# A mixture of experts whose weights' sums leave GpSimd and are kept in DRAM, with the first expert's first layer as a plain product

## The chip, the cores and the metric

The kernel runs on one core of one Trainium2 chip. The metric is device time in microseconds (us), the median of several executions. One further execution was taken with the hardware profiler; its span, from the first instruction to the last, is what the profile's rows divide. The engines are named as in the profile: PE is TensorE (PEld its loads of weights), DVE VectorE, ACT ScalarE, POOL GpSimd, SP the queue that issues DMAs.

## The reference

Attention over q, k, v (4 batches, 8 heads, 1152 positions, 64 features), with the queries averaged in pairs, gives 2304 tokens of 512 features. They go through a dense mixture of eight experts (each 512 to 1024 to 512) and then through a second mixture, a soft one with 32 slots.

```python
def _moe_ref(x, w_gate, w1, w2):
    N, D = x.shape                      # 2304, 512
    E = w_gate.shape[1]                 # 8
    logits = x @ w_gate
    P = np.exp(logits - logits.max())
    for _ in range(8):
        P /= P.sum(1, keepdims=True) + 1e-09
        P /= P.sum(0, keepdims=True) + 1e-09
        P *= N / E
    out = np.zeros((N, D), dtype=np.float32)
    for e in range(E):
        h = np.maximum(x @ w1[e], 0.0)  # 512 -> 1024
        ye = h @ w2[e]                  # 1024 -> 512
        out += P[:, e:e + 1] * ye
    return out
```

All values are float32. The kernel computes each large product from a high and a low half of both operands (three matmuls: high x high, high x low, low x high). Making the halves is called a split: ScalarE casts the high half (`hi`, L459, or L519, L634), VectorE subtracts it for the low half (`lo`, L462, or L520, L635).

## The kernel before

**Attention** runs first, over 32 heads in 288 slots of nine to a head (18 slots are a pair of heads). ScalarE's exponentials are L221, GpSimd adds up their rows (L227), and L244, L246 and L250 to L260 normalise. A table `hooks` puts other work at numbered slots, counted back from attention's end: in the kernel before, parts of `prep` (sums and splits of the tokens, whose results are stored in DRAM), sums and splits of expert 0's weights, and `v_store`, which makes sums of expert 0's second weights and stores them.

**The first mixture** has nine blocks of 256 tokens, eight of them in four pairs u = 0 to 3 and one single, u = 4, taken in the order 0, 1, 4, 2, 3. For experts 0 to 6 both layers are products in Strassen's manner: a pair's first layer is made of seven products of forms of w1 (11, 12, S2, S3, 22, S1, S4, of which S1 to S4 are sums of w1's quarters) with forms of the tokens (B11 to B22, T1 to T4, read back from DRAM by `load_x`, L565, into three buffers). Each is two chunks of 12 matmuls (`chunk`, L661). A block's second layer is seven products of 12 matmuls (`product`, L706) of forms of the hidden values (`h_sum`, L628, `h_split`, L634 and L635) with seven forms of w2 (V, j = 0 to 6). L718 multiplies by the gate's P and adds to the output. L670, L680, L684 and L689 bring the first layer's products out of PSUM. The last expert is plain in both layers (`g1`, L737 to L739, and `g2`).

The order is written out by hand: a list `items` of chunks and products, which are TensorE's steps, and `at(k, ...)`, which puts other engines' work behind step k, with `late` as its order there. `merge` writes a stretch of steps from a text ("c" a chunk, "p" a product): a pair's chunks stand among the products of the block before, then six chunks stand together, then the rest stand among the products of the pair's first block. `starts[e, u]` is a pair's first step, `bounds[e, u]` (r) the last of its six chunks together. Each engine works through its own queue in order, SP's DMAs included.

**Weights at a change of expert.** While pair u = 3 of expert e runs, `stage_w` and `stage_v` load the eight quarters of expert e+1's weights into the staging buffers (pool `stg`, five of 4 KB a partition); GpSimd makes four sums of w1 (`w_sum`, L452) and four of w2 (`v_sum`, L483) in place, and each form is split into its tile behind the last matmul of the expert before that reads that tile. The splits lie at steps r-8 to r+36. GpSimd also makes two of the four `h_sum`s of each block.

Of the kernel before, what the change touches and what calls it, by code (L numbers as in the profile page):

```python
# [357 lines left out]
def tile_attention__moe__softmoe(ctx, tc, q, k, v, w_gate, w1, w2, phi, m2_w1, m2_w2, out):  # L358
# [105 lines left out]
    def w_hi(e, form):  # L464
        Wt[e, form] = w_tile(form)
        hi(Wt[e, form], staged[e, HOME[form]])

    def w_lo(e, form):
        lo(Wt[e, form], staged[e, HOME[form]])

    def w_split(e, form):
        w_hi(e, form)
        w_lo(e, form)
# [6 lines left out]
    def v_sum(e, k, eng=None):  # L480
        q = [staged[e, x] for x in ((0, 0), (0, 1), (1, 0), (1, 1))]
        dst, a, b = {1: (q[0], q[1], q[0]), 2: (q[0], q[3], q[0]), 3: (q[1], q[3], q[1]), 4: (q[2], q[2], q[0])}[k]
        (eng or nc.vector).tensor_tensor(out=dst, in0=a, in1=b, op=ALU.subtract)  # L483

    VHOME = [(0, 0), (1, 0), (0, 0), (0, 0), (0, 1), (1, 1), (1, 0)]
    Vd = {}

    def v_store(k):
        v_sum(0, k)
        j = {1: 3, 2: 2, 3: 4, 4: 6}[k]  # L490
        Vd[j] = dram_p.tile([128, 1024], F32, name=f"vd{j}")
        nc.sync.dma_start(out=Vd[j], in_=staged[0, VHOME[j]])

# [3 lines left out]
    def v_hi(e, j):  # L497
        if e:
            V[e, j] = v_tile(j)
        hi(V[e, j], staged[e, VHOME[j]])  # L500

    def v_lo(e, j):
        lo(V[e, j], staged[e, VHOME[j]])

    def v_raw(j, t):
        staged[0, j] = t
        if j in Vd:
            nc.sync.dma_start(out=t, in_=Vd[j])
        else:
            nc.sync.dma_start(out=t.rearrange("p (c d) -> p c d", c=4), in_=quarter(0, VHOME[j]))  # L510

    def v0_split(j):
# [813 lines left out]
```

## Time and profile before

| | us |
|---|---|
| median of three executions | 2233.35 |
| lowest and highest | 2231.29, 2235.98 |
| the profiled execution | 2234.42 |
| its span, first to last instruction | 2232.6 |

The mean granted clock of TensorE in the span is 0.982 of full speed. Times within the span are counted from its start. A matmul's recorded length holds its way through the array, so matmuls overlap in the rows: the pace is read from one start to the next.

### The profile page before, as it was taken

The numbers are of one execution on the slowest core, as the hardware profiler recorded it, in microseconds if no ns is written. First come the engines' busy times: TensorE is split into PE (matmuls) and PEld (weight loads), VectorE is DVE, ScalarE is ACT, GpSimd is POOL, SyncE is SP. The second block draws the span as 40 slices with busy tenths as digits, with TensorE's granted clock in tenths as the row PEclk, the third lists the DMA queues.
The fourth block names the chain that finished last, engine by engine and source line by source line (L and its number), as shares of the span: only waits on it lengthen the run. The fifth ranks groups of instructions, "written<-read, shape, count | busy, mean of one in ns | idle before, by whom it ended". The sixth has DMA issues, their size and how long they took to land.

```text
span 2232.6 us, 40083 instructions
## 1 busy us (share of the span) xinstructions
PE 2124.9 (95%) x16119; PEld 1899.6 (85%) x16119; DVE 1448.3 (65%) x2421; ACT 971.8 (44%) x1994; POOL 724.3 (32%) x479
## 2 busy tenths in 40 slices
PE   7999999999999999999999999999999999999997
PEld 5677666666899899989999999999999999999863
DVE  5878787885666865785576478557647745544461
ACT  3555555555544543443344344345434534311232
POOL 5888786777011411331141133114113311000000
PEclk9999999999999999999999999999999999999998
DMA  8745656524344322422333242233224223487568
GB/s 205 179 117 150 163 142 182 128 67 144 123 174 152 116 98 77 142 95 76 133 114 105 76 142 95 77 132 123 95 85 137 97 80 110 169 323 257 208 225 266
DMA packets 153065, 311.49 MB, mean 140 GB/s; under 512 B 47920, under 2 KB 86832, under 8 KB 150832
## 3 DMA queue, kind: packets, MB, share of 16 engines
q1 hardware_dynamic: 152880, 308.93, 43.7%
q8 instruction: 128, 2.10, 0.4%
q14 instruction: 57, 0.47, 0.1%
HBM read 250.69 MB, written 25.17 MB: 124 GB/s over the span
## 4 chain that ended last, share of the span: by engine, by line
PE 69%; DVE 20%; ACT 5%; issue 3%; DMA 1%; SPq 1%; POOL 1%; ACTq 0%; DVEq 0%; POOLq 0%
PE y L706 20%; PE g L661 12%; PE seed L661 9%; PE o L234 5%; PE se L218 5%; DVE ho L635 5%; PE S L189 4%; ACT ho L634 2%; DVE v L462 2%; DVE acc L718 2%; DVE w L462 2%; DVE m L190 2%; DVE hr L689 1%; PE g L738 1%; PE g L739 1%
## 5 line engine op out<-in xcount | busy, mean ns | idle before, releaser
L706 PE MATMUL y<-v,ho 128*128 128x256 f32 x5292 | 704.5, 288 | 47.6 <-DVE acc L718 33.4
L706 PEld LDWEIGHTS y<-v,ho 128*128 128x128 f32 x5292 | 669.6, 195 | 61.2 <-issue 33.8
L661 PE MATMUL g<-xs,w 128*128 128x256 f32 x3360 | 442.7, 284 | 0.0
L661 PEld LDWEIGHTS g<-xs,w 128*128 128x128 f32 x3360 | 422.4, 193 | 1.4 <-issue 1.3
L227 POOL TENSOR_TENSOR acc<-acc,e 128x576 f32<-128x576 f32 x224 | 329.1, 1469 | 70.8 <-ACT e L221 60.2
L628 POOL TENSOR_TENSOR ht<-hr,ht 128x512 f32<-128x512 f32 x63 | 84.9, 1347 | 685.0 <-DVE ho L635 679.6
L635 DVE TENSOR_TENSOR ho<-ht,ho 128x512 fp32r<-128x512 f32 x252 | 232.6, 925 | 107.9 <-ACT ho L634 105.4
L190 DVE TENSOR_REDUCE m<-S 128x1 f32<-128x384 f32 x432 | 229.7, 547 | 74.3 <-PE S L189 61.7
L635 DVE TENSOR_TENSOR ho<-hr,ho 128x512 fp32r<-128x512 f32 x189 | 162.5, 860 | 162.8 <-ACT ho L634 162.6
L718 DVE SCALAR_TENSOR_TENSOR acc<-y,P,acc 128x256 f32<-128x256 f32 x378 | 181.1, 480 | 133.1 <-PE y L706 131.2
L221 ACT ACTIVATE e<-se 128x288 f32<-128x288 f32 x576 | 207.1, 412 | 96.7 <-PE se L218 89.5
L661 PE MATMUL seed<-xs,w 128*128 128x256 f32 x2016 | 247.7, 283 | 0.0
L661 PEld LDWEIGHTS seed<-xs,w 128*128 128x128 f32 x2016 | 244.2, 192 | 0.8 <-ACT v L459 0.4
L218 PE MATMUL se<-q,kd 128*128 128x288 f32 x1152 | 223.5, 312 | 7.2 <-ACT e L221 5.7
L218 PEld LDWEIGHTS se<-q,kd 128*128 128x128 f32 x1152 | 179.1, 192 | 21.0 <-ACT e L221 14.5
L634 ACT CAST ho<-ht 128x512 fp32r<-128x512 f32 x252 | 149.5, 615 | 104.9 <-DVE ht L628 71.3
L628 POOL TENSOR_TENSOR ht<-hr 128x512 f32<-128x512 f32 x63 | 84.2, 1337 | 300.5 <-ACT hr L670 300.5
L234 PE MATMUL o<-e,vr 128*64 128x288 f32 x1152 | 174.0, 424 | 0.0
L189 PE MATMUL S<-kd,q 128*128 128x384 f32 x384 | 150.0, 395 | 18.1 <-DVE m L190 16.4
L670 ACT ACTIVATE hr<-hr 128x512 f32<-128x512 f32 x112 | 69.9, 632 | 201.6 <-DVE hr L689 201.6
L189 PEld LDWEIGHTS S<-kd,q 128*128 128x128 f32 x384 | 74.3, 194 | 82.3 <-issue 31.9
L684 ACT COPY hr<-seed 128x512 f32<-128x512 f32 x112 | 65.8, 587 | 158.0 <-PE seed L661 157.9
(182 smaller groups left out, 2580.4 us busy)
## 6 DMA issues: line engine op xcount, KB each, us to landing
stg<-in_moe_w_dram SPq DMA_DIRECT2D x64, 512.0 KB, 6.0
xs<-xd0B SPq DMA_DIRECT2D x37, 512.0 KB, 3.2
xs<-xd1B SPq DMA_DIRECT2D x37, 512.0 KB, 3.3
xs<-xd2B SPq DMA_DIRECT2D x37, 512.0 KB, 3.3
xs<-xd3B SPq DMA_DIRECT2D x37, 512.0 KB, 3.6
kd<-kp SPq DMA_DIRECT2D x32, 576.0 KB, 6.3
xs<-xd0T SPq DMA_DIRECT2D x28, 512.0 KB, 3.3
xs<-xd1T SPq DMA_DIRECT2D x28, 512.0 KB, 3.2
```

Source lines behind the costliest of these rows:

```text
L189: nc.tensor.matmul(ps, lhsT=w, rhs=r[:, 384 * n:384 * n + 384], start=True, stop=True)
L190: nc.vector.tensor_reduce(out=M_[ph][:, x, n:n + 1], in_=ps, axis=AX.X, op=ALU.max)
L218: nc.tensor.matmul(ps, lhsT=kd[:, z, 128 * c:128 * c + 128], rhs=y[:, h, g], start=z == 0, stop=z == 1)
L221: nc.scalar.activation(out=e[:, g], in_=ps, func=AF.Exp, scale=1.0 / 16)
L227: nc.gpsimd.tensor_tensor(out=acc_[ph], in0=acc_[ph], in1=e, op=ALU.add)
L234: nc.tensor.matmul(O_[ph][64 * g:64 * g + 64, :288], lhsT=raws["v"][pi][:, h, c, :], rhs=E_[ph, c][:, g], start=c == 0, stop=c == 8,)
L628: (eng or nc.vector).tensor_tensor(out=o, in0=a, in1=b, op=op)
L634: nc.scalar.copy(o[:, 0], p)
L635: nc.vector.tensor_tensor(out=o[:, 1], in0=p, in1=o[:, 0].bitcast(F32), op=ALU.subtract)
L661: nc.tensor.matmul(o, lhsT=w[:, a, kk, cols], rhs=x[:, b, kk], start=begin, stop=kk == 1 and z == 2, skip_group_check=not first or f2 > 0,)
L706: nc.tensor.matmul(ps, lhsT=o[:, x, c], rhs=v[:, w, c], start=first and c + z == 0, stop=c + z == 5, skip_group_check=not first,)
L718: nc.vector.scalar_tensor_tensor(out=y, in0=ps, scalar=p, in1=y, op0=ALU.mult, op1=ALU.add)
```

## The change

- GpSimd does no sums in the first mixture. `h_sum` s3 and s4 go to VectorE, each put one step or less ahead of its split.
- The eight sums of an expert's weights are made an expert ahead, on VectorE (`fsum`): for expert e+1 while pairs u = 1 (w1) and u = 2 (w2) of expert e run (for expert 1, in blocks 5 to 7 of expert 0). They are stored in DRAM (`fstore`). At the change of expert all 14 forms are loaded one by one (`stage_f`), the sums from DRAM and the others as they are.
- The splits of the 14 forms are spread over r-8 to r+31 by a table (`FORMS`, and `FORMS0` for expert 1): load, high half and low half each have a step.
- Expert 0's first layer is one plain product (`plain`, four steps of 24 matmuls a block), from a plain split of its weights in four parts (`p_split`; part 0 in attention, 1 to 3 behind it) and of the tokens (`x0_split`, per block, whose halves are also stored as B11 to B22). Blocks follow one another, a block's four steps among the seven products of the block before.
- Attention's hooks keep only the load and split of one part of the weights, `x0_split(0)`, three more loads and the load of the gate's weights. T1 to T4 and BD are made in expert 0's blocks 1 to 4 and 7; expert 0's seven forms of w2 from four raw quarters in its first eight slots; the gate's steps lie in the slots of expert 0, with one more step between a row sum and its column sum.
- The staging pool has four buffers for five, the pool of token and output tiles ten for nine.

```diff
@@ pools, sums and splits
-    xa_p = ctx.enter_context(tc.tile_pool(name="xa", bufs=NBLK))
-    stg_p = ctx.enter_context(tc.tile_pool(name="stg", bufs=5))
+    xa_p = ctx.enter_context(tc.tile_pool(name="xa", bufs=NBLK + 1))
+    stg_p = ctx.enter_context(tc.tile_pool(name="stg", bufs=4))
...
-    def w_sum(e, name, eng=None):
-        q = {x: staged.get((e, x)) for x in W1Q}
+    Fd = {}
+
+    def fsum(e, name):
         dst, a, b, op = {
             "S3": ("11", "11", "21", ALU.subtract),
             "S1": ("21", "21", "22", ALU.add),
-            "S2": ("11", "22", "11", ALU.subtract),
-            "S4": ("12", "12", "11", ALU.subtract),
+            "S2": ("22", "22", "11", ALU.subtract),
+            "S4": ("12", "12", "22", ALU.subtract),
+            3: ((0, 0), (0, 1), (0, 0), ALU.subtract),
+            4: ((0, 1), (1, 1), (0, 1), ALU.subtract),
+            2: ((1, 1), (1, 1), (0, 0), ALU.subtract),
+            6: ((1, 0), (1, 0), (1, 1), ALU.subtract),
         }[name]
-        (eng or nc.vector).tensor_tensor(out=q[dst], in0=q[a], in1=q[b], op=op)
+        t = staged[e, dst]
+        nc.vector.tensor_tensor(out=t, in0=staged[e, a], in1=staged[e, b], op=op)
+        staged[e, name] = t
+
+    def fstore(e, name):
+        d = Fd[e, name] = dram_p.tile([128, 1024], F32, name=f"fd{e}{name}")
+        nc.sync.dma_start(out=d, in_=staged[e, name])
+
+    def stage_tile(e, name):
+        if name in (0, "S4"):
+            return xa_p.tile([128, 1024], F32, tag="xa", name="stg")
+        return stg_p.tile([128, 1024], F32, tag="stg", name="stg")
+
+    def stage_f(e, name):
+        if (e, name) in Fd:
+            t = staged[e, name] = stage_tile(e, name)
+            nc.sync.dma_start(out=t, in_=Fd[e, name])
+        elif name in VQ:
+            stage_v(e, VQ[name], stage_tile(e, name))
+            staged[e, name] = staged[e, VQ[name]]
+        else:
+            stage_w(e, name)
...
+    def x0_split(i):
+        u, t = divmod(i, 2)
+        for h in range(2):
+            pool, tag, bufs = (m_p, "hr", 4) if i and h else (wp_p, "x", 3)
+            x = X0[i, h] = pool.tile([128, 2, 2, 256], F32R, tag=tag, name="xs", bufs=bufs)
+            z = x.rearrange("p z k n -> p z (k n)")
+            part = xa[i].rearrange("p k n -> p (k n)")[:, 512 * h:512 * h + 512]
+            nc.scalar.copy(z[:, 0], part)
+            nc.vector.tensor_tensor(out=z[:, 1], in0=part, in1=z[:, 0].bitcast(F32), op=ALU.subtract)
...
@@ attention's hooks
-    for h, step, fs in ((-210, 8, prep(0)), (-134, 4, prep(1)), (-36, 8, X2[:4])):
-        for n, f in enumerate(fs):
-            hooks[h + step * n] = [f]
-            hooks[h + step * n + 2] = [store_x]
-    for h, f in {
...
-        -102: lambda: [stage_w(0, q) for q in ("22", "11", "21", "12")],
-        -92: lambda: w_split(0, "11"),
-        -88: lambda: w_sum(0, "S3"),
-        -80: lambda: w_split(0, "S3"),
-        -72: lambda: w_sum(0, "S1"),
-        -64: lambda: w_sum(0, "S2"),
-        -56: lambda: w_split(0, "S2"),
-        -48: lambda: w_split(0, "12"),
-        -40: lambda: w_sum(0, "S4"),
-        -24: lambda: load_x(3),
-        -286: lambda: [stage_v(0, q) for q in Q],
-        -276: lambda: v_store(1),
-        -266: lambda: v_store(3),
-        -256: lambda: v_store(2),
-        -246: lambda: v_store(4),
-    }.items():
+    PTAG = ("S3", "22", "S1", "S4")
...
+            {-56: [lambda: stage_p(0, 0)],
+             -48: [lambda: p_split(0, 0, PTAG[0])],
+             -40: [lambda: x0_split(0)],
+             -24: [lambda: stage_p(0, 1), lambda: stage_p(0, 2), lambda: stage_p(0, 3)],
...
@@ the plain first layer
+    def plain(i, fp):
+        ps = pg.tile([128, 512], F32, tag="g", name="g")
+        w = Wt[0, fp].rearrange("p z (k f) -> p z k f", k=4)
+        for f2 in range(2):
+            o = ps[:, 256 * f2:256 * f2 + 256]
+            c = slice(128 * f2, 128 * f2 + 128)
+            for kk in range(4):
+                xk = X0[i, kk // 2][:, :, kk % 2]
+                nc.tensor.matmul(o, lhsT=w[:, 0, kk, c], rhs=xk[:, 0], start=kk == 0, stop=False)
+                nc.tensor.matmul(o, lhsT=w[:, 0, kk, c], rhs=xk[:, 1], start=False, stop=False)
+                nc.tensor.matmul(o, lhsT=w[:, 1, kk, c], rhs=xk[:, 0], start=False, stop=kk == 3)
+        nc.scalar.activation(out=quad(i, fp // 2, fp % 2, True), in_=ps, func=AF.Relu)
@@ behind attention
+    for q in Q:
+        nc.sync.dma_start(out=staged[0, q].rearrange("p (c d) -> p c d", c=4), in_=quarter(0, q))
+    for p in range(1, 4):
+        p_split(0, p, PTAG[p])
@@ the order of the work
         at(s12, (h_sum, i, "s1"), (h_sum, i, "s2"))
-        at(s12, (h_sum, i, "s3", nc.gpsimd), (h_sum, i, "s4", nc.gpsimd))
         at(s1, (h_split, i, 1))
         for j, k in enumerate(others):
             at(k, (h_split, i, 2 + j), late=0.5)
+        at(max(others[0], others[1] - 1), (h_sum, i, "s3"), late=0.6)
+        at(others[1], (h_sum, i, "s4"), late=0.7)
...
+        for c in "pfppfppfppf" if i else "ffff":
+            if c == "f":
+                item(plain, i, fp)
+                fp += 1
+            else:
+                pos.append(item(product, 0, i - 1, len(pos)))
+        if i:
+            second(0, i - 1, pos, [base[i - 1] + (6 if i > 1 else 3), b - 1, b - 1, b, b, b + 2, b + 3, b + 5])
...
+    FORMS = (
+        ("11", -14, -8, -7), ("12", -12, -6, -5), ("S2", -9, -3, -2), ("S3", -7, -1, 0), ("22", -5, 1, 14), ("S1", -2, 5, 17),
+        (0, 2, 14, 19), (1, 6, 16, 20), (2, 8, 18, 22), (3, 15, 20, 23), (4, 18, 23, 24), ("S4", 20, 25, 26), (5, 21, 26, 27),
+        (6, 23, 28, 31),
+    )
...
-            for form, d in (("11", -8), ("12", -6), ("S3", -1), ("22", 2), ("S1", 5), ("S2", 12), ("S4", 27)):
-                at(r + d - (form == "22"), (w_hi, n, form), late=form != "22")
-                at(r + d + 1, (w_lo, n, form), **late)
-            for form, d in (("S3", -6), ("S1", -4), ("S2", 1), ("S4", 5)):
-                at(r + d, (w_sum, n, form, nc.gpsimd), **late)
-            for q, d in zip(Q, (-4, 4, 7, 14)):
-                at(r + d, (stage_v, n, q), **late)
-            for k, d in ((1, 16), (3, 18), (2, 23), (4, 25)):
-                at(r + d, (v_sum, n, k, nc.gpsimd), **late)
-            for j, d in ((0, 14), (1, 19), (3, 21), (4, 23), (2, 25), (5, 33), (6, 35)):
-                at(r + d, (v_hi, n, j), **late)
-                at(r + d + 1, (v_lo, n, j), **late)
+            for name, st, h, l in FORMS if e else FORMS0:
+                at(r + st, (stage_f, n, name), **late)
+                at(r + h, (f_hi, n, name), late=0.2 if name == "22" else 1)
+                at(r + l, (f_lo, n, name), **late)
+            if e:
+                jobs = ((starts[e, 1] + 4, bounds[e, 1] - 5, 1), (starts[e, 2] - 2, bounds[e, 2] - 5, 1))
+            else:
+                jobs = ((base[5] + 2, base[5] + 6, 2), (base[6] + 3, base[6] + 7, 2))
+            for (s, d, w), raws, names, stage in zip(jobs, (W1Q, Q), (WS, VS), (stage_w, stage_v)):
+                at(s, *((stage, n, q) for q in raws), **late)
+                for j, name in enumerate(names):
+                    at(d + w * j, (fsum, n, name), **late)
+                    at(d + w * j + 1, (fstore, n, name), **late)
...
+    for i in range(1, NBLK):
+        at(base[i - 1] + 2, (x0_split, i), **late)
+        at(base[i - 1] + (4 if i > 1 else 3), (x0_store, i), **late)
...
+    first = [
+        ((v_split, 0), (v_sum, 1)),
+        ((v_split, 1), (v_sum, 3)),
+        (),
+        ((v_split, 3), (v_sum, 2)),
+        ((v_split, 2), (v_sum, 4)),
+        ((v_split, 4),),
+        ((v_split, 5),),
+        ((v_split, 6),),
+    ]
+    for k, fs in zip(slots, first):
+        at(k, *fs, late=0.8)
```

## Rows read from the trace of the kernel before

**Rows 1.** Windows cut by stage: length, each engine's busy us (instructions), granted clock, DMA.
```profile
557.94:760.65 202.71, 192.25 (x1569) 185.47 (x1568) 138.50 (x237) 102.14 (x190) 32.59 (x21) 0.97 0.41 146
...
955.49:1150.59 195.10, 187.84 (x1525) 186.07 (x1525) 126.28 (x176) 83.32 (x137) 45.99 (x26) 0.98 0.31 106
...
1734.16:1922.95 188.79, 185.12 (x1525) 183.52 (x1525) 116.09 (x170) 79.91 (x134) 34.35 (x22) 1.00 0.29 98
1922.95:2232.60 309.65, 289.14 (x2112) 236.10 (x2110) 136.35 (x271) 66.63 (x173) 3.73 (x4) 0.97 0.71 250
```

**Rows 2.** Windows of one expert by pair, the same columns: u=0, u=1, u=3.
```profile
955.50:1000.80 45.30, 42.05 (x337) 40.96 (x337) 38.30 (x46) 23.79 (x37) 15.23 (x8) 0.99 0.27 93
1000.80:1041.30 40.50, 40.50 (x338) 40.38 (x337) 22.57 (x37) 16.68 (x30) 5.79 (x5) 1.00 0.26 92
...
1104.10:1150.60 46.50, 42.89 (x339) 42.71 (x338) 33.24 (x42) 20.68 (x33) 16.84 (x9) 0.93 0.46 159
```

**Rows 3.** Timeline of TensorE at a change: start, length, instructions, idle before.
```profile
942.14 3.04 PE L706 MATMUL y<-v,ho 128*128 128x256 f32 x24
945.02 1.60 PE L661 MATMUL g<-xs,w 128*128 128x256 f32 x12
950.23 5.46 PE L706 MATMUL y<-v,ho 128*128 128x256 f32 x24 [3.61 <-DVE acc L718]
```

**Rows 4.** Timeline of VectorE at the same change.
```profile
937.64 0.69 DVE L635 TENSOR_TENSOR ho<-ht,ho 128x512 fp32r<-128x512 f32 x1
...
939.45 1.22 DVE L462 TENSOR_TENSOR w<-stg,w 128x1024 fp32r<-128x1024 f32 x1
...
946.33 3.36 DVE L462 TENSOR_TENSOR w<-stg,w 128x1024 fp32r<-128x1024 f32 x1
949.61 0.47 DVE L718 SCALAR_TENSOR_TENSOR acc<-y,P,acc 128x256 f32<-128x256 f32 x1
```

**Rows 5.** Timeline of GpSimd at the same change.
```profile
943.00 5.61 POOL L452 TENSOR_TENSOR stg<-stg 128x1024 f32<-128x1024 f32 x2
```

**Rows 6.** Timeline of TensorE behind that change.
```profile
971.97 1.67 PE L706 MATMUL y<-v,ho 128*128 128x256 f32 x12 [1.14 <-DVE acc L718]
...
997.35 1.79 PE L706 MATMUL y<-v,ho 128*128 128x256 f32 x13 [1.23 <-DVE acc L718]
```

**Rows 7.** Windows of attention, ScalarE's L221 alone: length, busy us (count), clock, DMA.
```profile
60.95:528.40 467.45, 181.19 (x505) 0.99 0.57 143
...
125.70:156.90 31.20, 12.95 (x37) 1.00 0.53 124
...
220.20:256.80 36.60, 13.10 (x37) 1.00 0.56 146
...
462.60:496.10 33.50, 12.89 (x36) 1.00 0.35 81
```

**Rows 8.** VectorE's groups in expert 0: busy us, mean ns, idle before.
```profile
L635 DVE TENSOR_TENSOR ho<-ht,ho 128x512 fp32r<-128x512 f32 x32 | 26.6, 834 | 17.2 <-ACT ho L634 17.0
L635 DVE TENSOR_TENSOR ho<-hr,ho 128x512 fp32r<-128x512 f32 x25 | 20.0, 800 | 18.6 <-ACT ho L634 18.5
...
L718 DVE SCALAR_TENSOR_TENSOR acc<-y,acc 128x256 f32<-128x256 f32 x24 | 10.0, 418 | 4.9 <-PE y L706 4.7
...
L823 DVE TENSOR_TENSOR P<-P,cr 128x144 f32<-128x144 f32 x7 | 5.0, 720 | 0.2
...
L821 DVE TENSOR_SCALAR cr<-cs 128x8 f32<-128x8 f32 x7 | 1.1, 158 | 0.0
```

**Rows 9.** Timeline of VectorE at attention's end, the last normalisation.
```profile
558.59 1.97 DVE L250 RECIPROCAL rs<-rs 128x144 f32<-128x144 f32 x2 [6.40 <-ACT rs L246]
...
561.54 0.19 DVE L260 TENSOR_TENSOR x<-o,rs 64x32 f32<-64x32 f32 x1
```

**Rows 10.** DMA issues from 1101 to 1108 us: KB each, median us to landing.
```profile
stg<-in_moe_w_dram SPq DMA_DIRECT2D x4, 512.0 KB, 7.4
xs<-xd3T SPq DMA_DIRECT2D x1, 512.0 KB, 3.4
```

**Rows 11.** SP's waits in one expert, 955 to 1150 us: total, times, longest.
```profile
SPq L429 <- DVE w L462: 7.0, 3, 3.4
```

More of the change, by code (lines that the diff above doesn't have):

```diff
@@ L462, in lo, with f_hi, f_lo @@
         (eng or nc.vector).tensor_tensor(out=u[:, 1], in0=t, in1=u[:, 0].bitcast(F32), op=ALU.subtract)
[L464 to L473, printed above, removed]
+    def f_hi(e, name):
+        if name in range(7):
+            t = V[e, name] = v_tile(name)
+        else:
+            t = Wt[e, name] = w_tile(name)
+        hi(t, staged[e, name])
+    def f_lo(e, name):
+        lo(V[e, name] if name in range(7) else Wt[e, name], staged[e, name])
     def p_split(e, p, tag):
@@ L478, in p_split, with v_sum, v_split @@
         lo(t, staged[e, p])
[L480 to L492, printed above, removed]
+    def v_sum(k):
+        q = [staged[0, x] for x in ((0, 0), (0, 1), (1, 0), (1, 1))]
+        if k == 4:
+            staged[0, "t4"] = stg_p.tile([128, 1024], F32, tag="stg", name="t4")
+        dst, a, b = {1: (q[0], q[1], q[0]), 2: (q[0], q[3], q[0]), 3: (q[1], q[3], q[1]), 4: (staged.get((0, "t4")), q[2], q[0])}[k]
+        nc.vector.tensor_tensor(out=dst, in0=a, in1=b, op=ALU.subtract)
     def v_tile(j):
         return wpools["m"].tile([128, 2, 1024], F32R, tag=f"v{j}", name="v", bufs=1)
[L497 to L512, printed above, removed]
+    def v_split(j):
+        t = staged[0, ((0, 0), (1, 0), (0, 0), (0, 0), (0, 1), (1, 1), "t4")[j]]
         V[0, j] = v_tile(j)
-        hi(V[0, j], staged[0, j])
-        lo(V[0, j], staged[0, j])
+        hi(V[0, j], t)
+        lo(V[0, j], t)
     def x_split(u, op, part):
@@ L522, in x_split, with x0_store @@
         stores.append(lambda: nc.sync.dma_start(out=Xd[u, op], in_=t.rearrange("p z n -> p (z n)").bitcast(F32)))
+    X0 = {}
+    def x0_split(i):
[7 more added lines that the diff above has]
+            nc.vector.tensor_tensor(out=z[:, 1], in0=part, in1=z[:, 0].bitcast(F32), op=ALU.subtract)
+    def x0_store(i):
+        u, t = divmod(i, 2)
+        for h in range(2):
+            op = f"B{h + 1}{t + 1}"
+            Xd[u, op] = dram_p.tile([128, 1024], F32, name=f"xd{u}{op}")
+            nc.sync.dma_start(out=Xd[u, op], in_=X0[i, h].rearrange("p z k n -> p (z k n)").bitcast(F32))
     stores = []
@@ L1074, in merge @@
         return pos
-    pend, bounds, starts = None, {}, {}
-    for e in range(E - 1):
+    pend, bounds, starts, base, slots = None, {}, {}, [], []
+    for i in range(NBLK):
+        b = len(items)
+        base.append(b)
+        pos, fp = [], 0
+        for c in "pfppfppfppf" if i else "ffff":
[6 more added lines that the diff above has]
+            second(0, i - 1, pos, [base[i - 1] + (6 if i > 1 else 3), b - 1, b - 1, b, b, b + 2, b + 3, b + 5])
+        slots += [b + d for d in ((0, 1, 3, 4, 6, 7, 9, 10) if i else range(4))]
+    pend = (0, NBLK - 1, len(items) - 1, "zero")
+    for e in range(1, E - 1):
         for u in ORDER[e]:
@@ L1138, in tile_attention__moe__softmoe @@
             at(r + 15, (p_split, n, 4, "v0"), **late)
-    late = dict(late=True)
-    for k, form in ((1, "22"), (3, "S1"), (5, "S4")):
-        at(k, (w_split, 0, form), **late)
-    for k, j in ((4, 0), (6, 1), (7, 2), (9, 6), (11, 3), (13, 4), (15, 5)):
-        at(k, (v0_split, j), **late)
-    for j, f in enumerate([*prep(4), *X2[4:], *prep(3)]):
-        at(starts[0, 1] + 2 + 3 * j, (f,), **late)
-        at(starts[0, 1] + 4 + 3 * j, (store_x,), **late)
-    at(starts[1, 0], (const2,), late=True)
+    T = [f for u in (0, 1, 2, 3, 4) for f in prep(u)]
+    where = [base[1] + d for d in (2, 4, 6, 8)] + [base[2] + d for d in (4, 7, 10, 12)] + [base[3] + d for d in (4, 7, 10, 13)]
+    where += [base[4] + d for d in (4, 6, 8, 10)] + [base[7] + 4]
+    for k, f in zip(where, T):
+        at(k, (f,), **late)
+        at(k + 2, (store_x,), **late)
+    for i in range(1, NBLK):
+        at(base[i - 1] + 2, (x0_split, i), **late)
+        at(base[i - 1] + (4 if i > 1 else 3), (x0_store, i), **late)
+    at(base[7] + 4, (load_x,), **late)
+    at(base[8] + 2, (load_x,), **late)
+    at(base[8] + 10, (load_x,), **late)
+    first = [
[10 more added lines that the diff above has]
+        at(k, *fs, late=0.8)
+    at(starts[1, 1], (const2,), late=True)
     gate = gate_steps()
@@ L1153, in tile_attention__moe__softmoe @@
         if f is not None:
-            at(5 + 2 * n if n < 18 else 8 + 2 * n, (f,), **late)
+            at(slots[n + 3], (f,), late=0.9)
     for f, after in items:
```

79 lines of the change are left out of this document (40 added, 39 removed).

## The prediction, made before the kernel was run

> **What bounds the kernel now.** I read the table of stages first, cut where the first matmul of each expert's first layer starts. TensorE is busy nearly throughout, VectorE for some two thirds, so what matters is where TensorE is held up. The parts of the sum: attention 557.94 us; expert 0 of the first MoE 202.71; experts 1 to 5 together 973.51 (760.65 to 1734.16, of which one expert's row stands for five: 195.10); expert 6 188.79; the dense last expert, the second MoE and the output 309.65 [rows 1].
>
> Next, one expert cut by block pair [rows 2]. It holds 768 matmuls of the first layer and 756 of the second. A run of 24 without a hole advances by 2.88 us (from 942.14 to 945.02), 0.12 us each, and a step of the schedule (12) by 1.44 [rows 3]. The 28 steps of a pair cost 40.3 us, the whole expert 1524 x 0.12 = 182.9. Pair u=1 takes 40.5: TensorE sets its pace and nothing else shows. The last pair, u=3, takes 46.5 and the next expert's first, u=0, 45.3: 6.2 + 5.0 = 11.2 us are lost at each change of expert, nearly all of the 12 above 182.9.
>
> How it is lost is seen in the timelines. TensorE stands 3.61 us until VectorE's L718, the add that empties a bank; then its next 24 matmuls take 5.46 us, where 24 take 3.04 elsewhere [rows 3]: after the stall the granted clock is at its lower level (1.2 GHz for 2.4), and that costs another 2.4. L718 takes 0.47 us itself. Ahead of it VectorE spent 3.36 us in a split of weights (L462) that took 1.22 seven us before [rows 4]. In that time GpSimd runs two sums of weights, 5.61 us without a break [rows 5]. The split reads two SBUF operands, as the sums do. Behind the change come smaller holes in TensorE, of 1.14 and 1.23 us among others, ended by the same L718 [rows 6], while GpSimd makes w2's sums.
>
> Last, attention, by ScalarE's exponentials (L221), 36 to a head pair of 18 slots. A pair without a hook takes 31.2 us, one with hooks of two sums and a split 36.6. The 14 pairs from 60.95 to 528.40 take 467.45 us; 14 x 31.2 is 436.8, so the hooks cost 30.6 [rows 7].
>
> **The change, part by part.**
>
> *Attention.* It loses 20 x_splits with their stores, eight token sums, four sums and four splits of w1, four sums of w2 with their stores. It gets one p_split (a cast and a subtraction of 1024), x0_split (two casts and two subtractions of 512) and four loads of 512 KB. A pair that now holds one split and one sum of w1 takes 33.5, 2.3 over 31.2 [rows 7]; I put the new work at 2.1 by it and the gain at 28.5. Bounds: 30.6 (the new work hides) and 24.3 (it costs three times as much). Attention ends at 529.4.
>
> *Expert 0.* Layer 1 becomes plain: 9 blocks x 96 = 864 matmuls for 768, +96 x 0.12 = 11.5 us that nothing hides. With 8 x 84 = 672 of layer 2 in the stage, 1536 x 0.12 = 184.3; the gate's matmuls, as now, I estimate at 10.6. So 195 without a hole; now it is 172.8 + 10.6 = 183.4 and takes 202.7, 19 us of it holes.
>
> New holes can come from VectorE. Its work there, at 0.69 us for 512 columns and 1.22 for 1024 [rows 4]: seven splits and four sums a block, eight blocks, 60.7; 24 adds at 0.42 [rows 8], 10.1; 16 halves of x0_split, 11.0; 34 instructions of prep, 23.5; 28 of 1024 columns (three p_splits, seven v_splits, four v_sums, eight fsums, six splits of expert 1), 34.2; the gate's nine groups, of which the first and the last are shown, 25.9 [rows 8], and some 4 of copies and maxima; attention's end 3.2. That is 172.6 of 195, 88%, where it is now 138.5 of 202.7 [rows 1]. On average it fits; at the start it does not. Counted from attention's end: its last normalisation ends at 3.8 [rows 9], p_splits 1 to 3 at 7.4, so the plain layer's second quarter, due at 2.9, waits 2. Then four of 1024 columns (12.3), x0_split (13.7), the next block's first split; the sums s1 and s2 and a second split, which wait for block 0's last ReLU at 15.2 (17.3); two of 1024 (19.7); two splits and two sums (22.5); and only then v_split(2), 23.7. The product that needs it is due at 11.5 + 2 + 1 (gate) + 1.44 + 2.88 + 1.44 = 20.3: a hole of 3.4, and one of about 1 behind it. Slow stretches of the clock after these I put at 3, from the 2.4 of [rows 3], and the fuller blocks 4 to 8 at 2.6. Together 12: expert 0 takes 207, 4.3 more than now. Bounds: 199 (the first hole and one slow stretch) and 216 (VectorE also keeps the 40.7 us for which it now waits ahead of L635 and L718 [rows 8], 172.6 + 40.7 = 213.3, and slow stretches of 3).
>
> *The change of expert.* GpSimd's sums go, 18 of 512 and 8 of 1024 columns an expert, 46 us [rows 1]. VectorE does 18 x 0.69 + 8 x 1.22 = 22.2 us in their place. Even if none of its stretched instructions became shorter, that is 126.3 + 22.2 = 148.5 of 183 us, 81%. The eight long sums lie at r-5 to r-2 of pairs u=1 and u=2, where six steps of the first layer stand together; what hides them is that TensorE needs little of VectorE there. Without that cover they would show with 9.8 us an expert. The 14 splits lie eight steps or more ahead of their first matmul (form 22's low half at r+14 for r+27, v6's at r+31 for r+39). SP gets 30 transfers of 512 KB in place of 8: eight raw loads, eight stores, 14 loads, all through the queue that also loads x. Four raw loads in one burst land in 7.4 us (median), the x tile ahead of them in 3.4 [rows 10]; the first sum comes seven steps (10.1 us) behind its burst for w1, thirteen for w2, so the data is there. Behind a load that waits for a staging buffer stand the x loads; such waits for L462 are 7.0 us an expert now, the longest 3.4 [rows 11]. x has three buffers, and two of them hold 5.8 us of matmuls. I take 1.5 us for what is left at each change of the 11.2, with bounds of 0 and 4 (the 3.4, rounded up for the clock). Experts 1 to 5: 973.5 - 5 x 9.7 = 925.0. Expert 6 has only the entry, 5.0 of which 0.8 stays: 188.8 - 4.2 = 184.6.
>
> A row shows VectorE waiting 17.2 us in all for ScalarE's casts at the head of its queue [rows 8]. The Trainium skill says on its page "TensorE: Matmul & The Clock Gate", section "Architectural detail: the array is 16× 32×32, not 1× 128×128", that ScalarE and VectorE take their queues strictly in order. By that rule a moved sum whose data is late would hold every add behind it, and the sum would come to rival 2's 2181; by the landing times it comes to 2157.
>
> *Unchanged.* The last stage, 309.65: the same instructions but for one tag.
>
> Sum: 529.4 + 207 + 925.0 + 184.6 + 309.65 = 2155.7 of span. The profiled execution took 2234.42, its span 2232.6, the median is 2233.35: 1.8 more and 1.1 less make 2156.4, say 2157.
>
> **Rivals.**
> 1. VectorE sets expert 0's pace. For it: 88%, in order, waiting for two engines. Against: between a block's last first-layer step and its second product lie 4.3 us, and the chain that must fit is 2.8. It gives 20 more: 2177.
> 2. Late transfers hold the change: a sum or a split waits for its data, or x for SP; 4 us more each time, 24 in all: 2181. For it: 30 transfers in one queue. Against: five steps or more from a load to its cast, eight or more from a split to its matmul.
> 3. The long head pairs have another cause than hooks, such as their key transfers, and stay: 22 more, 2179. Against: the pair without a hook at 31.2.
> 4. GpSimd was not the cause; the splits hold L718. The change keeps 9 of its 11.2, 7.5 more five times and 3.5 once: 2198. Against: 3.36 and 1.22 us for one instruction.
> 5. Slower than before: SP's queue. If each of the 30 transfers holds the x loads, and TensorE behind them, for 0.48 us, a change loses 14.3 us, 12.8 above my 1.5; six times that is the whole gain of 77. At 0.55 us the time is 2247.
>
> **How the numbers follow.** Chances: the forecast 0.62 (2143 to 2172), rivals 1 to 5 0.17, 0.11, 0.05, 0.02, 0.03. All bounds low: 2157 - 2.1 - 8 - 8.3 = 2138; all high: 2157 + 4.2 + 9 + 14 = 2184, and I take 2186, which leaves out rivals 4 and 5 and the ends of the others. The three executions spread by 0.2%, about what can be told from no change. Faster 0.96, same 0.01, slower 0.03.
>
> **What would show it.** Right: head pairs at 31.2 us nearly throughout and attention over near 529; in expert 0 holes mostly in the first 40 us; u=3 and u=0 within 2 us of 40.3; L462 and L635 at 1.22 and 0.69 us throughout the first MoE, where GpSimd is idle. Wrong: holes of TensorE behind VectorE in every block of expert 0; L565's loads issued late at a change; head pairs that stay at 33 to 38.

## The result and the profile after

The changed kernel takes 2150.41 us in the median of four executions (2150.05 to 2151.62); the kernel before, on the same chip, 2233.78. The ratio is 0.9628, 95% interval 0.9611 to 0.9645: 83.4 us or 3.7% faster. The prediction was 2157 in a range of 2138 to 2186.

The stages of the changed kernel's profiled execution (windows: length, busy us of PE, PEld, DVE, ACT and POOL with their counts, granted clock, DMA), to be set against [rows 1]:

```profile
0.00:529.54 529.54, 510.12 (x3300) 361.52 (x3300) 383.55 (x819) 293.39 (x787) 412.74 (x303) 1.00 0.54 127
529.54:739.13 209.59, 202.15 (x1662) 195.41 (x1661) 151.01 (x280) 99.82 (x185) 0.00 (x0) 0.98 0.41 151
...
923.37:1106.56 183.19, 183.16 (x1526) 182.95 (x1525) 127.49 (x203) 83.41 (x137) 0.00 (x0) 1.00 0.52 176
1656.11:1839.29 183.18, 183.15 (x1526) 182.94 (x1525) 113.63 (x191) 79.37 (x133) 0.00 (x0) 1.00 0.34 114
1839.29:2148.28 308.99, 288.75 (x2112) 235.18 (x2110) 136.53 (x273) 66.30 (x172) 1.92 (x2) 0.97 0.72 250
```

Attention is 28.4 us shorter, expert 0 6.9 longer, experts 1 to 5 together 56.5 shorter (739.13 to 1656.11, 916.98 for 973.51), expert 6 5.6, the last stage 0.7: 84.3 in all, the difference of the spans. An expert now takes 183.19, and 1524 matmuls at 0.12 us are 182.9.

The same expert by pair, against [rows 2]; u=0, u=1, u=2 and u=3:

```profile
923.37:964.00 40.63, 40.60 (x338) 40.39 (x337) 34.43 (x53) 23.28 (x36) 0.00 (x0) 1.00 0.47 156
964.00:1004.32 40.32, 40.32 (x338) 40.32 (x337) 27.91 (x46) 16.57 (x29) 0.00 (x0) 1.00 0.58 196
...
1025.92:1066.24 40.32, 40.32 (x338) 40.32 (x337) 27.23 (x43) 16.73 (x29) 0.00 (x0) 1.00 0.61 211
1066.24:1106.56 40.32, 40.32 (x338) 40.32 (x337) 27.40 (x45) 21.53 (x34) 0.00 (x0) 1.00 0.62 209
```

u=3 takes what its 336 matmuls take, u=0 0.3 us more. VectorE's work in u=1 has risen from 22.57 to 27.91 us by the sums put there, and TensorE does not show it. Where TensorE stood 3.61 us at the change [rows 3], its timeline has no hole:

```profile
1099.36 3.04 PE L725 MATMUL y<-v,ho 128*128 128x256 f32 x24
1102.24 1.60 PE L667 MATMUL g<-xs,w 128*128 128x256 f32 x12
1103.68 3.04 PE L725 MATMUL y<-v,ho 128*128 128x256 f32 x24
1106.56 1.60 PE L667 MATMUL g<-xs,w 128*128 128x256 f32 x12
```

The new line numbers of the old lines are L725 for L706, L667 for L661, L737 for L718, L640 and L641 for L634 and L635. The split of weights that once took 3.36 us [rows 4], now L488, by its line's view (count, then min, median and max in ns):

```profile
L488 DVE TENSOR_TENSOR w<-stg,w x50: 1211/1218/1331, 446.2 to 1980.4; 128x1024 fp32r<-128x1024 f32 x50
```

Attention's exponentials over the same 14 head pairs and over one pair without and one with a hook, against [rows 7]:

```profile
60.75:497.10 436.35, 180.27 (x503) 1.00 0.54 127
123.05:154.20 31.15, 12.91 (x37) 1.00 0.53 127
434.70:469.20 34.50, 12.86 (x37) 1.00 0.42 109
```

The 14 pairs take 436.35 us for 467.45, 31.2 a pair. The last pair shown holds most of what is left of the hooks.

In expert 0 TensorE's waits are few (waits: engine, line, waited for; total us, times, longest):

```profile
PE g L708 <- DVE w L488: 2.1, 1, 2.1
PE lg L397 <- ACT lg L392: 1.5, 1, 1.5
PE y L725 <- ACT acc L733: 1.4, 1, 1.4
...
PE y L725 <- DVE v L488: 0.8, 1, 0.8
```

SP now waits some 16.5 us an expert for VectorE where it waited 7.0 for the line of [rows 11] and 5.1 for GpSimd's sums; the longest wait is again 3.4, and TensorE never waits for an x tile.

### The profile page after: what moved, and what is told of

It is laid out like the page before. It is cut to its first block, busy times and chain, and to the rows that moved or that the text cites. A ratio compares the mean times of both kernels' runs of the same rounds, so it can differ in the third digit from the quotient of the medians.

```text
span 2148.3 us, 40255 instructions
## 1 busy us (share of the span) xinstructions
PE 2100.9 (98%) x16215; PEld 1890.3 (88%) x16215; DVE 1419.8 (66%) x2572; ACT 958.0 (45%) x1967; POOL 414.7 (19%) x305
## 4 chain that ended last, share of the span: by engine, by line
PE 70%; DVE 3%; ACT 1%; DMA 1%; issue 0%; SPq 0%; ACTq 0%; DVEq 0%
PE y L725 29%; PE g L667 16%; PE seed L667 9%; PE g L756 2%; PE g L757 2%; PE g L758 2%; PE y L777 1%; PE g L706 1%; PE y L778 1%; PE y L779 1%; PE g L708 1%; PE g L707 1%; PE f L1286 1%; PE f L1314 0%; DVE ho L641 0%; DMA m2w<-in_moe_w_dram 0%
## 5 line engine op out<-in xcount | busy, mean ns | idle before, releaser
L725 PE MATMUL y<-v,ho 128*128 128x256 f32 x5292 | 680.7, 284 | 6.0 <-DVE acc L737 1.9
L725 PEld LDWEIGHTS y<-v,ho 128*128 128x128 f32 x5292 | 654.2, 192 | 12.8 <-issue 5.5
L667 PE MATMUL g<-xs,w 128*128 128x256 f32 x2880 | 375.9, 283 | 0.0
L667 PEld LDWEIGHTS g<-xs,w 128*128 128x128 f32 x2880 | 359.0, 192 | 0.0
L737 DVE SCALAR_TENSOR_TENSOR acc<-y,P,acc 128x256 f32<-128x256 f32 x378 | 181.2, 480 | 118.6 <-PE y L725 116.0
L221 ACT ACTIVATE e<-se 128x288 f32<-128x288 f32 x576 | 207.0, 411 | 87.9 <-PE se L218 84.6
L641 DVE TENSOR_TENSOR ho<-hr,ho 128x512 fp32r<-128x512 f32 x189 | 130.2, 689 | 149.1 <-ACT ho L640 146.9
L667 PE MATMUL seed<-xs,w 128*128 128x256 f32 x1728 | 211.3, 283 | 0.0
L667 PEld LDWEIGHTS seed<-xs,w 128*128 128x128 f32 x1728 | 209.1, 192 | 0.0
L641 DVE TENSOR_TENSOR ho<-ht,ho 128x512 fp32r<-128x512 f32 x252 | 170.3, 686 | 51.3 <-ACT ho L640 49.0
L640 ACT CAST ho<-ht 128x512 fp32r<-128x512 f32 x252 | 150.2, 618 | 110.9 <-DVE ht L634 109.3
L634 DVE TENSOR_TENSOR ht<-hr 128x512 f32<-128x512 f32 x126 | 86.2, 684 | 54.5 <-ACT hr L676 31.8
L234 PEld LDWEIGHTS o<-e,vr 128*64 128x64 f32 x1152 | 69.9, 136 | 57.2 <-issue 28.7
L676 ACT ACTIVATE hr<-g 128x512 f32<-128x512 f32 x72 | 43.0, 597 | 165.2 <-PE g L667 165.1
```

Source lines behind the costliest of these rows:

```text
L221: nc.scalar.activation(out=e[:, g], in_=ps, func=AF.Exp, scale=1.0 / 16)
L234: nc.tensor.matmul(O_[ph][64 * g:64 * g + 64, :288], lhsT=raws["v"][pi][:, h, c, :], rhs=E_[ph, c][:, g], start=c == 0, stop=c == 8,)
L634: (eng or nc.vector).tensor_tensor(out=o, in0=a, in1=b, op=op)
L640: nc.scalar.copy(o[:, 0], p)
L641: nc.vector.tensor_tensor(out=o[:, 1], in0=p, in1=o[:, 0].bitcast(F32), op=ALU.subtract)
L667: nc.tensor.matmul(o, lhsT=w[:, a, kk, cols], rhs=x[:, b, kk], start=begin, stop=kk == 1 and z == 2, skip_group_check=not first or f2 > 0,)
```

## Experiments

Theory A was that of the prediction: GpSimd's sums stretch VectorE's instructions, and that holds TensorE. Theory B: the change of expert is crowded, whichever engine makes the sums. The runs led to a third, C: VectorE's place in time is what is short at the change, and both its own work there and GpSimd's sums beside it take from that. Runs 1, 3, 4 and 7 came first; 2, 5, 6 and 8 were made with C at hand.

**1. All sums on VectorE.** The kernel before, with the sums of weights at their old steps and s3 and s4 at those of the changed kernel:

```diff
-        at(s12, (h_sum, i, "s3", nc.gpsimd), (h_sum, i, "s4", nc.gpsimd))
...
+        at(max(others[0], others[1] - 1), (h_sum, i, "s3"), late=0.6)
+        at(others[1], (h_sum, i, "s4"), late=0.7)
...
-                at(r + d, (w_sum, n, form, nc.gpsimd), **late)
+                at(r + d, (w_sum, n, form), **late)
...
-                at(r + d, (v_sum, n, k, nc.gpsimd), **late)
+                at(r + d, (v_sum, n, k), **late)
```

> The kernel before with one thing changed: all of GpSimd's sums in the first mixture (four of w1, four of w2 for each of experts 1 to 6, h_sum s3 and s4 of every block) are made by VectorE at their old steps, s3 and s4 at the changed kernel's steps. Attention, expert 0, the splits' steps and the loads are as before. Theory A, GpSimd's sums hold VectorE's instructions with two SBUF operands: the loss at a change (11.2 us over pairs u=3 and u=0) falls to 3 or less, L462 and L635 take 1.22 and 0.69 us, and the time is about 2186 (2233.8 less 6 x 8). Theory B, the crowd at the change is the cause, whichever engine makes the sums: VectorE has 22 us more to do there, the loss stays at 8 or more, and the time is 2215 or above.

Measured: 2199.82 us in the median of four, ratio 0.9861 (0.9845 to 0.9878), between the two forecasts. Windows of u=0, of u=3 and of a whole expert:

```profile
1130.17:1172.59 42.42, 41.02 (x339) 40.47 (x338) 36.74 (x52) 23.79 (x37) 0.00 (x0) 1.00 0.31 100
...
1274.83:1320.68 45.85, 42.55 (x339) 41.97 (x337) 33.13 (x50) 20.56 (x33) 0.00 (x0) 0.96 0.47 162
...
1130.17:1320.68 190.51, 185.81 (x1527) 184.68 (x1525) 125.78 (x200) 83.29 (x137) 0.00 (x0) 0.99 0.33 108
```

GpSimd does nothing here, no split of weights is stretched, and still a change loses 5.5 + 2.1 = 7.6 us of the former 11.2. A alone falls: giving GpSimd's sums to VectorE at the same place is worth a third. Of TensorE's waits at this change 3.5 us of 4.6 are for L718 as before, the longest 2.4. How that one comes about, at the change ahead of these windows, in VectorE's rows, ScalarE's and TensorE's:

```profile
1120.34 1.22 DVE L452 TENSOR_TENSOR stg<-stg 128x1024 f32<-128x1024 f32 x1
1121.47 0.68 DVE L689 TENSOR_TENSOR hr<-g,hr 128x512 f32<-128x512 f32 x1
1123.37 0.69 DVE L635 TENSOR_TENSOR ho<-ht,ho 128x512 fp32r<-128x512 f32 x1 [1.21 <-ACT ho L634]
1123.97 1.22 DVE L462 TENSOR_TENSOR w<-stg,w 128x1024 fp32r<-128x1024 f32 x1
1125.11 0.48 DVE L718 SCALAR_TENSOR_TENSOR acc<-y,P,acc 128x256 f32<-128x256 f32 x1
```
```profile
1122.19 0.63 ACT L670 ACTIVATE hr<-hr 128x512 f32<-128x512 f32 x1 [3.58 <-DVE hr L689]
```
```profile
1125.73 4.60 PE L706 MATMUL y<-v,ho 128*128 128x256 f32 x24 [2.37 <-DVE acc L718]
```

A sum of weights (L452) stands ahead of L689, for which ScalarE waits before it makes the next cast; VectorE in turn stands 1.21 us for that cast (L634), and a split of weights (L462) is ahead of L718. No instruction is slow: it is the order in VectorE's queue, and the way through ScalarE and back, that TensorE waits for.

**2. The short sums alone.** The kernel before with only the first of these edits; GpSimd keeps the sums of weights.

> The kernel before with h_sum s3 and s4 alone on VectorE; GpSimd keeps the eight sums of weights at the change. It parts the 31.6 us of the run with all sums on VectorE. Theory C: the long sums of weights do the harm, so little comes back: 2220 to 2234. If the 126 short sums were the harm: 2205 or below.

Measured: 2209.00 (one execution; 2230.02 before), between the two forecasts. An expert takes 192.27 us, against 195.1 before and 190.5 in run 1:

```profile
0.00:552.83 552.83, 515.10 (x3300) 362.25 (x3300) 422.61 (x856) 303.71 (x808) 423.17 (x303) 1.00 0.59 149
...
942.47:1134.74 192.27, 185.97 (x1526) 184.72 (x1525) 128.18 (x195) 83.33 (x137) 21.56 (x8) 0.99 0.32 108
```

I had expected little of it; the short sums, on VectorE and at their later steps, give 2.8 us an expert, the long ones 1.8 more. Of the 25.5 us between this profiled execution and that of [rows 1], 5.1 are not the edit's: attention, whose code is the same, is shorter by that much (see the last section).

**3. Splits not spread.** The changed kernel with the old steps in its table, sums still made ahead:

```diff
-        ("11", -14, -8, -7), ("12", -12, -6, -5), ("S2", -9, -3, -2), ("S3", -7, -1, 0), ("22", -5, 1, 14), ("S1", -2, 5, 17),
-        (0, 2, 14, 19), (1, 6, 16, 20), (2, 8, 18, 22), (3, 15, 20, 23), (4, 18, 23, 24), ("S4", 20, 25, 26), (5, 21, 26, 27),
-        (6, 23, 28, 31),
+        ("11", -14, -8, -7), ("12", -12, -6, -5), ("S3", -9, -1, 0), ("22", -7, 1, 3), ("S1", -5, 5, 6), ("S2", -2, 12, 13),
+        (0, 2, 14, 15), (1, 2, 19, 20), (3, 4, 21, 22), (4, 8, 23, 24), (2, 15, 25, 26), ("S4", 17, 27, 28),
+        (5, 22, 33, 34), (6, 24, 35, 36),
...
```

> The changed kernel with the table of splits put back to the old steps (low half one step behind the high half, v5 and v6 at r+33 to r+36), sums still made an expert ahead on VectorE and loaded. Theory A: GpSimd is idle, so the place of the splits matters little: at most 1 us more at each of five changes, 2150 to 2156. Theory B: the spreading did a good part of it: 4 us or more at each, 2170 or above.

Measured: 2156.86 in the median of four, ratio 0.9665 (0.9650 to 0.9679), just above the range that A gave. An expert takes 184.15 us:

```profile
924.77:1108.92 184.15, 183.67 (x1526) 183.12 (x1525) 126.90 (x203) 83.69 (x137) 0.00 (x0) 1.00 0.51 175
```

So the spreading is worth 1.0 us an expert. The big step, from 190.5 to 184.15, is between run 1 and this: the sums stand elsewhere, and the forms are loaded one by one at new steps. No run parted these two.

**4. The sums made ahead, on GpSimd.**

```diff
-        nc.vector.tensor_tensor(out=t, in0=staged[e, a], in1=staged[e, b], op=op)
+        (nc.gpsimd if e > 1 else nc.vector).tensor_tensor(out=t, in0=staged[e, a], in1=staged[e, b], op=op)
```

> The changed kernel with the sums made ahead on GpSimd instead of VectorE for experts 2 to 6, at the same steps in pairs u=1 and u=2. Theory A: GpSimd is busy 8 x 2.7 us an expert again and VectorE's two-operand instructions are stretched there, but TensorE needs little of VectorE at these steps: 0 to 1.5 us a pair, 2150 to 2165. If GpSimd's sums cost as much anywhere as at the change (some 11 us an expert): about 2200. Theory B: no change, 2150.

Measured: 2192.87 (one execution): 42 us are lost again. Nearly all of it is paid in one of the two pairs. Windows of u=1 (w1's sums) and u=2 (w2's):

```profile
973.68:1014.62 40.94, 40.58 (x338) 40.37 (x337) 24.74 (x42) 16.57 (x29) 9.59 (x4) 1.00 0.57 193
1036.22:1084.32 48.10, 43.29 (x338) 42.74 (x337) 30.52 (x39) 16.73 (x29) 10.53 (x4) 0.93 0.50 178
```

The timelines say why. GpSimd in u=2:

```profile
1040.34 10.76 POOL L458 TENSOR_TENSOR stg<-stg 128x1024 f32<-128x1024 f32 x4 [42.02 <-DMA stg<-in_moe_w_dram]
```

It began when its data had landed, 4 us into the pair, and not at the six steps, of which the first begins at 1059.84: `at` puts an instruction behind others of its engine, and GpSimd has no others. So the sums lay among the products of the block before. VectorE beside them, and TensorE:

```profile
1040.44 2.85 DVE L641 TENSOR_TENSOR ho<-ht,ho 128x512 fp32r<-128x512 f32 x1 [0.75 <-ACT ho L640]
1043.22 0.47 DVE L737 SCALAR_TENSOR_TENSOR acc<-y,P,acc 128x256 f32<-128x256 f32 x1
1043.61 2.48 DVE L634 TENSOR_TENSOR ht<-hr 128x512 f32<-128x512 f32 x1
1046.01 2.86 DVE L641 TENSOR_TENSOR ho<-ht,ho 128x512 fp32r<-128x512 f32 x1
```
```profile
1048.93 1.46 PE L725 MATMUL y<-v,ho 128*128 128x256 f32 x10 [1.75 <-DVE ho L641]
1053.19 6.82 PE L725 MATMUL y<-v,ho 128*128 128x256 f32 x36 [2.80 <-DVE acc L737]
```

Instructions of 0.69 us take up to 2.86 beside a sum of GpSimd; L737, which reads PSUM and one SBUF operand, keeps its 0.47. Four instructions are stretched, of which three are shown, and each of them ends 0.55 us behind the end of one of GpSimd's four sums. The Trainium skill says on its page "SBUF — State Buffer", section "Who interferes with whom", that a VectorE instruction with two SBUF inputs contends with a GpSimd one that reads SBUF, for a pair of ports that the two share as an exclusive lock. By that rule the first split waits for the rest of the sum that began 0.1 us before it, 2.40 us long, and does its own work behind it; the trace agrees with its 2.85. The stretch is real, then, and it costs 7.8 us where TensorE waits for products' splits and 0.6 where it doesn't (48.10 and 40.94 us for 40.32 in the changed kernel).

**5. The same, with w2's raw quarters loaded later.**

```diff
-                jobs = (..., (starts[e, 2] - 2, bounds[e, 2] - 5, 1))
+                jobs = (..., (starts[e, 2] + 4, bounds[e, 2] - 5, 1))
```

> As the run with the sums made ahead on GpSimd (2192.9), but w2's raw quarters are loaded six steps later (step 4 of pair u=2 for step -2), as w1's are in u=1, so that GpSimd can begin only where the six first-layer steps stand. Theory C, it is the place in time and not the engine that decides, since GpSimd starts as soon as its data has landed: u=2 falls from 48 us to 41 or less, as u=1 has it, and the time to about 2155 (2150.4 plus up to 1 us in each of ten pairs, less what doesn't show). If GpSimd's sums cost much wherever they lie: u=2 stays at 45 or more and the time above 2175.

Measured: 2157.56 (one execution), 35 us better than run 4, with one number of the edit changed. u=1 and u=2:

```profile
964.80:1005.72 40.92, 40.57 (x338) 40.37 (x337) 24.71 (x42) 16.56 (x29) 9.61 (x4) 1.00 0.57 193
1027.32:1068.72 41.40, 40.55 (x338) 40.38 (x337) 23.81 (x39) 16.73 (x29) 9.93 (x4) 1.00 0.60 205
```

u=2 falls by 6.7 us, to 41.4 for the 41 expected, and GpSimd's 20 us of long sums an expert cost 1.7 us when they lie in the right place. That place is not quite the one of the expectation. GpSimd begins 6.4 us ahead of the six steps, which start at 1044.25; but VectorE then has one instruction with two SBUF operands left, and the next comes at 1051.35:

```profile
1037.81 10.16 POOL L458 TENSOR_TENSOR stg<-stg 128x1024 f32<-128x1024 f32 x4 [48.38 <-DMA stg<-in_moe_w_dram]
```
```profile
1038.75 2.01 DVE L641 TENSOR_TENSOR ho<-hr,ho 128x512 fp32r<-128x512 f32 x1 [0.91 <-ACT ho L640]
```

TensorE's only wait behind it is 0.85 us. C holds, then: what counts is which of VectorE's results TensorE still needs while GpSimd works.

**6. The short sums on GpSimd in the changed kernel** (`nc.gpsimd` in the two `at` lines of run 1).

> The changed kernel with h_sum s3 and s4 of every block on GpSimd, 126 instructions of 1.3 us. Theory C: they lie between products, where VectorE's splits are wanted, but each is half as long as a sum of weights and VectorE has 40 percent of its time free in a plain pair: 0 to 0.4 us a pair in u=1 and u=2 and up to 2 at a change, 2150 to 2168. Were GpSimd's time the price, 18 x 1.3 us an expert would give back 10 us an expert, 2210.

Measured: 2154.43 (one execution), in the range of C. An expert takes 183.59 us, 0.4 more. The 18 short sums, which cost 2.8 us an expert beside a crowded change (run 2, at other steps), cost 0.4 where the change isn't crowded.

**7. Token sums back in attention.** T1 to T4 of pairs 0 and 1:

```diff
...
+    for h, fs in ((-178, prep(0)), (-118, prep(1))):
+        for n, f in enumerate(fs):
+            hooks[h + 8 * n] = [f]
+            hooks[h + 8 * n + 2] = [store_x]
...
-    T = [f for u in (0, 1, 2, 3, 4) for f in prep(u)]
+    T = [f for u in (2, 3, 4) for f in prep(u)]
```

> The changed kernel with the token sums and splits T1 to T4 of pairs 0 and 1 put back into attention's hooks (eight hooks from slot -178 and from -118 on, eight slots apart), and taken out of expert 0's blocks 1 and 2. If such hooks are what made attention's head pairs long: attention ends 5 to 10 us later than 529.5 with pairs of 33 to 36 us in these stretches, expert 0 is 2 to 5 us shorter, 2151 to 2158 in all. If the long pairs had another cause (rival 3 of the prediction): attention still ends at 529.5 and the time falls to about 2147.

Measured: 2158.75 (one execution). Attention's end moves by 11.3 us, a little more than the 5 to 10 expected, and expert 0 becomes 3.9 shorter. Two of the pairs with these hooks, as windows of the exponentials, are long again, one with the 36.6 of [rows 7]:

```profile
216.35:252.90 36.55, 13.10 (x37) 1.00 0.56 144
314.75:348.80 34.05, 13.04 (x37) 1.00 0.57 143
```

The hooks are the cause; rival 3 falls.

**8. The start in another order.** The places were chosen by the waits of expert 0 shown above; the core of the edit:

```diff
-    PTAG = ("S3", "22", "S1", "S4")
+    PTAG = ("S3", "S2", "S1", "S4")
...
-            {-56: [lambda: stage_p(0, 0)],
-             -48: [lambda: p_split(0, 0, PTAG[0])],
-             -40: [lambda: x0_split(0)],
+            {-36: [lambda: stage_p(0, 0)],
+             -14: [lambda: p_split(0, 0, PTAG[0])],
+             -8: [lambda: x0_split(0)],
+             2: [lambda: p_split(0, 1, PTAG[1])],
...
-    where = [base[1] + d for d in (2, 4, 6, 8)] + ...
+    where = [base[1] + d for d in (6, 8, 9, 12)] + ...
...
-        ((v_split, 1), (v_sum, 3)),
-        (),
         ((v_split, 3), (v_sum, 2)),
+        ((v_split, 1), (v_sum, 3)),
         ((v_split, 2), (v_sum, 4)),
+        (),
```

> The changed kernel with the start of expert 0 put in another order: the first split of the plain weights and x0_split(0) 34 and 32 slots later, in attention's last slots, where VectorE has little to do; the second part's split before the last normalisation (its tile is that of form S2, which expert 1 then fills after 22); v_split(3) and v_sum(2) one slot earlier; the first product's split a step earlier; the token sums of pairs 0 to 2 a few steps later, BD's one step later. By the holes in the profile (2.1 and 2.7 us in attention's hooks and at the second plain step, 0.6 + 0.2 + 0.8 + 1.5 in block 1, 0.8 in block 4, 1.4 in block 7, two slow stretches of 1.7) it gains 4 to 9: 2141 to 2146. If TensorE is held by VectorE's whole load in expert 0 and not by these places, the holes move and it stays within 2 us of 2150.

Measured: 2138.41 us in the median of five, ratio 0.9585 (0.9570 to 0.9600): the fastest of all. Attention ends 2.2 us earlier and expert 0 takes 201.07 for 209.59:

```profile
0.00:527.35 527.35, 508.33 (x3299) 360.61 (x3299) 383.02 (x820) 293.62 (x788) 412.99 (x303) 1.00 0.54 128
527.35:728.42 201.07, 199.53 (x1663) 193.87 (x1662) 149.45 (x279) 99.16 (x184) 0.00 (x0) 0.99 0.43 158
```

VectorE does the same work (149.45 us for 151.01) in less time, so its load does not set expert 0's pace, and rival 1 falls: single places did. The gain is 12.0 us for the 4 to 9 expected, 10.7 of it in these two stages by the profiles. Which of the shifts gave how much was not parted.

## Why the prediction was right, by its steps

*Attention.* Predicted end 529.4, measured 529.54. That the hooks are the cause holds by run 7. That the size fits to 0.1 us is in part luck: of the 30.6 us that I gave to the hooks, 5.6 were stretches at the lower clock behind their holes, which come in one execution and not in another (last section). Against run 2's attention, 552.83 us with the same code, the gain is 23.3 and not 28.4.

*Expert 0.* Predicted 207, measured 209.59. Of the plain layer's holes the one at the second quarter was 2.09 us for 2, by VectorE's split (L488) as worked out. That of v_split(2) was 0.78 for 3.4: the split ended 25.0 us behind attention's end for 23.7, but TensorE came to its product only at 24.3, for 20.3. Two holes weren't foreseen. ScalarE stood 4.29 us at the cast of T3 (L523), whose sum came late in VectorE's queue, and with it the gate's copy, which cost 1.52 us of TensorE. And in block 7 the cast of BD began only when a store of w2's sums had landed, at 710.03, and given one of the four staging buffers back: VectorE stood 4.0 us for it, and TensorE 1.42 for L733, behind it in ScalarE's queue.

```profile
558.57 0.62 ACT L523 CAST xt<-xs 128x512 fp32r<-128x512 f32 x1 [4.29 <-DVE xs L563]
...
710.10 0.62 ACT L523 CAST xt<-xs 128x512 fp32r<-128x512 f32 x1 [5.81 <-DMA stg<-in_moe_w_dram]
```

The second row names a load as what it waited for; by the times of landing it was the store, which landed 0.07 us before the cast began. All holes are 7.4 us. Two stretches of 3.5 us at the lower clock (granted 0.52 and 0.51), behind the holes of 2.09 and 1.52, cost some 3.1. With the 195 that is 205.5. The rest lies in some fifty intervals from one matmul's start to the next that are about 0.1 us longer than the usual 0.12, most of them beside the gate's matmuls.

One term of this part was sized wrongly without harm to the sum: VectorE's work was put at 172.6 us, 88% of the stage, and measured 151.01, or 72%. The lengths in the rows, which I added up, overlap in VectorE's queue too (the changed kernel's L641 at 551.50 and L634 at 552.10 start 0.60 us apart and are 0.68 and 0.69 long), 13.1 us in all; and the gate's groups, read while GpSimd worked beside them, fell from 25.9 us to 19.1. So rival 1 had less for it than the 88% that I gave.

*The change of expert.* Predicted 1.5 us left, measured 0.3, and experts 1 to 5 took 917.0 for 925.0: the largest error of the sum. Some 6 of these 8.0 us are the term of the change, sized too high; the pairs between the changes, which I left as they were, became shorter too (in the expert shown by 1.1 us). The step behind the term was right in what it removes and too narrow in why. "In that time GpSimd runs two sums" is a cause of the hole, as run 4's rows show once more, but by itself it is the smaller part. An expert goes from 195.1 to 192.3 with the short sums on VectorE, to 190.5 with the long ones, to 184.15 with the sums made ahead and the forms loaded (run 3), to 183.19 with the splits spread. Moving the long sums out of the change does more than moving them off GpSimd; run 5 shows that on GpSimd they do nearly as well there.

*SP's queue.* Thirty transfers in place of eight held TensorE nowhere at a change: rivals 2 and 5 did not come about. The prediction took from the Trainium skill, page "TensorE: Matmul & The Clock Gate", section "Architectural detail: the array is 16× 32×32, not 1× 128×128", that ScalarE and VectorE take their queues strictly in order. At the changes no sum was late, since the data lay there in time; in expert 0 the trace agrees with it, in the two holes that weren't foreseen (1.52 and 1.42 us of TensorE behind a late cast). Rival 4, that the change keeps 9 of 11.2, falls with the result, but not all of its cause: in run 1, with the sums on VectorE and GpSimd idle, 7.6 of the 11.2 stay. The last stage was 308.99 for 309.65.

## What to carry to other kernels

Ask of a stall not only which instruction was slow but how much that engine had to do in that stretch: here a helper engine's work, taken over in the same place, gave back a third, and moved to a stretch in which the bound engine asks for nothing it gave back nearly all, on either engine. An instruction on an otherwise idle engine starts when its data is there; its place in the program doesn't hold it back, its load does (run 4's sums ran 19.5 us ahead of their step). After such a change the next holes stand at single places (a cast behind a late sum, a buffer behind a store), and a few steps' shift of each was worth 11 us here in all by the profiles.

## What the runs showed of the hardware

The same holes do not always bring the lower clock. In [rows 1]'s execution the granted clock of three of attention's head pairs fell to 0.92 to 0.96 of full speed (windows of the exponentials; the clock follows the count):

```profile
319.90:357.90 38.00, 12.97 (x36) 0.92 0.60 168
357.90:393.70 35.80, 13.14 (x36) 0.93 0.73 186
393.70:427.80 34.10, 12.74 (x36) 0.96 0.47 111
```

In run 2, with the same code in attention and the holes where they were (TensorE waits 7.7 us in these pairs for 7.3, the longest 2.1 both times), the same pairs:

```profile
320.40:356.40 36.00, 12.86 (x36) 1.00 0.63 172
356.40:389.90 33.50, 12.91 (x36) 1.00 0.76 204
389.90:422.70 32.80, 12.69 (x36) 1.00 0.50 115
```

They are 2.0, 2.3 and 1.3 us shorter than in that execution. Why the clock stayed up was not followed. The executions of the kernel before spread from 2226.4 to 2236.0 us in these runs, so a difference of 5 us between two single executions shows little by itself.
